# Where the late weight buffers start: 448 instead of 128 modulo 512 bytes, and steps of 64 bytes between units

## The chip, the cores and the metric

One core of a Trainium2 chip runs the whole program. The metric is the device time of one execution in microseconds, as the median of several runs.

## The reference

Attention over two sequences, then two feed-forward layers over the 1152 tokens that it gives:

```python
# attention: 2 batches, 8 heads, 576 tokens, 64 per head
scores = q @ k.T / 8, kept in a window of 32 (heads 0-3), or of 32 steps of 4 (heads 4-7)
attn = softmax(scores) @ v
x = attn as (1152, 512)
# layer 1
h = x @ w_in                       # 512 -> 2048
x = (h * tanh(softplus(h))) @ w_out   # 2048 -> 512
# layer 2: four experts, weighted by p = domain_probs / sum
for e in range(4):
    out += p[:, e] * (relu(x @ w1[e]) @ w2[e])   # 512 -> 1024 -> 512
```

## The kernel before, in words

Nearly all numbers are 32 bits wide. To keep the products exact enough at TensorE's fast 32-bit type, each operand is split in two parts, a high part (`xh`, `wxh`, `gh`, ...) and a low part (`xl`, `wxl`, `gl`, ...), and each product is three matmuls: high by high, high by low, low by high.

The order of all instructions is written out by hand (`tc.manual_schedule()`), and tiles get their places in the order in which they are declared. Pool `big` holds what lives through the whole kernel: `xh` and `xl` (18432 bytes a partition each), `wxh` and `wxl` (16384 each), `gh` and `gl` (5120 each), three buffers `raw0` to `raw2` for loads (4104 bytes, rounded up to 4128), `prob`, `psum_e`, a tile `pad` of 192 bytes that nothing reads or writes, and `scr` (18432). In the built program `xh` begins at 128 modulo 512 bytes; so do the tiles up to `raw0`, since all their sizes are multiples of 512. `raw1` begins at 160 and `raw2` at 192, and after `pad` the tile `scr` is at 128 again.

Behind `big` stands the pool `ap1` of the attention (`kk`, `qq`, `vP`, `vD`, the loaded `nat` tiles, `pr`, `pT`, `xn`). When the attention is done it is closed (`att.close()`), and the pool `wpb` takes the same bytes with the late buffers: `late0` and `late1` (1024 columns), `late2` and `late3` (11264 columns each: high and low parts) and `late4` (640). All five begin at 128 modulo 512.

There are three stages:

- **Attention**, ten units of up to 128 tokens (`Unit`, `att_step`). Beside it the weights of layer 1 are loaded and decoded (`dec_load`, `dec_dve`, `dec_act`): a DMA into one of four buffers (`raws` and a piece of `scr`), two VectorE and two ScalarE operations and a subtraction on GpSimd for each half unit.
- **Layer 1** (`Step1`). A unit is 128 of the 2048 hidden columns: 512 columns of `w_in` and 512 of `w_out`. Units 0 to 3 stand in `wxh`/`wxl`, unit 4 in `late0`/`late1`, and units 5 to 15 in `late2`/`late3`, one after the other (`unit_tiles`). The tokens go in three groups of 512, 320 and 320. `Step1.first` (line 566) multiplies by `w_in`, with the unit as the stationary operand and the tokens (`xh`, `xl`) moving; `Step1.second` (line 590) multiplies by `w_out`, with the unit stationary and the activations (`gh`, `gl`) moving. Each step runs 12 matmuls for one unit in `first` and 12 in `second`; in groups of 320 columns a step has two units.
- **Layer 2** (`Group`). Four pairs of blocks of an expert stand in `late2`/`late3`, `PW` columns apart: `prep_a` writes the first 768 columns, `prep_s` the next 1024 (sums and differences of blocks, for seven products in place of eight), `w2_hi` and `w2_lo` the last 1024 (w2). Tokens go in two sets with 256 and 320 columns a matmul. `Group.prod` (line 786) has a block of 128 columns from `late2`/`late3` as the stationary operand. `Group.second` (line 861) has 512 columns of w2 in `late2`/`late3` as the moving operand and `gh`/`gl`, `wxh`/`wxl` or `late0`/`late1` as the stationary one.

Slices of columns start at multiples of 128 columns (512 bytes), save the moving slices of the groups and sets with 320 columns, of which every second one starts 256 bytes on.

Of the kernel before, what the change touches and what calls it, by code (L numbers as in the profile page):

```python
# [8 lines left out]
F32 = mybir.dt.float32  # L9
F32R = mybir.dt.float32r  # L10
# [13 lines left out]
def kernel(  # L24
# [22 lines left out]
    NUA = 4  # L47
# [4 lines left out]

    SETS = ((0, 256), (512, 320))
    GW = 640
    PW = 2816
    EXP, MISH = "exp_and_friends", "mish"

    big = ctx.enter_context(tc.tile_pool(name="big", bufs=1))
# [23 lines left out]
    raws = [big.tile([128, 4104], U8, name=f"raw{n}") for n in range(3)]  # L82
    prob = big.tile([128, NT // 128, NE], F32, name="prob")
    psum_e = big.tile([128, NT // 128], F32, name="psum_e")
    big.tile([128, 48], F32, name="pad")

    scr = big.tile([128, NT // 128 * DM], F32, name="scr")
    hbuf = [scr[:, GW * n:GW * (n + 1)] for n in (0, 1)]
# [19 lines left out]
    late = []  # L108

    def unit_tiles(u):  # L110
        n = slice(1024 * u, 1024 * (u + 1))
        if u < NUA:
            units[u] = (wxh[:, n], wxl[:, n])
        elif u == NUA:
            units[u] = late[0:2]
        else:
            n = slice(1024 * (u - NUA - 1), 1024 * (u - NUA))
            units[u] = (late[2][:, n], late[3][:, n])

    halves = sorted(((u, p) for u in range(NF1) for p in range(2)), key=lambda h: 2 * h[0] + (2.5 if h[1] else 0))  # L120
# [42 lines left out]
    def dec_act():  # L163
        n = ndec[0]
        h = half_at(n)
        if h:

            kw = kwbuf[n % 3]
            ACT.activation(kw.bitcast(F16)[:, 1:1024:2], kw.bitcast(F32), AF.Copy)
        h = half_at(n - 1)  # L170
        if h:
            u, part = h
            if part == 0:
                unit_tiles(u)
            w, (hi, lo) = kwbuf[(n - 1) % 3].bitcast(F32), (t[:, part_cols(part)] for t in units[u])
            ACT.activation(hi, w, AF.Copy)
            POOL.tensor_tensor(out=lo, in0=w, in1=hi.bitcast(F32), op=ALU.subtract)
            dec_load()
        ndec[0] += 1
# [365 lines left out]
    class Step1:  # L545
# [27 lines left out]
        def split(self):  # L573
            ACT.activation(self.ghi, self.hc, AF.Copy)  # L574
            DVE.tensor_tensor(out=self.glo, in0=self.hc, in1=self.ghi.bitcast(F32), op=ALU.subtract)  # L575
# [29 lines left out]
    for n in (0, 1):  # L605
        o = 2 * GW * (n + 1)
# [114 lines left out]
    def prep_a(n):  # L721
        o = PW * (n % NP2)
        r = stage1.rearrange("p (c f m) -> p c f m", c=4, f=2)
        a12 = [w[:, o:o + 512].rearrange("p (c m) -> p c m", c=4) for w in late[2:4]]
        a22 = [w[:, o + 512:o + 768].rearrange("p (c m) -> p c m", c=2) for w in late[2:4]]
        split(*a12, r[:, :, 0], DVE)
        split(*a22, r[:, 2:4, 1], DVE)
        a11, a12, a21, a22 = blocks()
        POOL.tensor_tensor(out=a22, in0=a21, in1=a22, op=ALU.add)  # L729
        POOL.tensor_tensor(out=a21, in0=a11, in1=a21, op=ALU.subtract)  # L730
        POOL.tensor_tensor(out=a11, in0=a22, in1=a11, op=ALU.subtract)
        POOL.tensor_tensor(out=a12, in0=a12, in1=a11, op=ALU.subtract)

    def prep_s(n):
        o = PW * (n % NP2) + 768
        split(late[2][:, o:o + 1024], late[3][:, o:o + 1024], stage1, DVE)
        load_w1(n + 1)
        ready.add(("s", n))

    def w2_hi(n):  # L740
        o = PW * (n % NP2) + 1792
        ACT.activation(late[2][:, o:o + 1024], stage2, AF.Copy)  # L742

    def w2_lo(n):
        o = PW * (n % NP2) + 1792
        hi, lo = (t[:, o:o + 1024] for t in late[2:4])
        POOL.tensor_tensor(out=lo, in0=stage2, in1=hi.bitcast(F32), op=ALU.subtract)  # L747
        load_w2(n + 1)
        ready.add(("w2", n))
# [5 lines left out]
    def amat(name, p, k):  # L755

        o = PW * p
        o += {"A11": 128 * k, "A12": 256 + 128 * k, "A22": 512 + 128 * k, "S2": 768 + 256 * k, "S3": 896 + 256 * k,
# [3 lines left out]
    class Group:  # L762
# [90 lines left out]
        def second(self, f, which=slice(None)):  # L853
            assert ("w2", self.e * NP2 + self.p) in ready
            o = PW * self.p + 1792 + 512 * f
            wh, wl = (w[:, o:o + 512] for w in late[2:4])
# [103 lines left out]
    u1.x_lo()  # L960
    att.close()
    wpb = ctx.enter_context(tc.tile_pool(name="wpb", bufs=1))
    late += [wpb.tile([128, n], F32R, name=f"late{i}") for i, n in enumerate((1024, 1024, 11264, 11264))]
    late.append(wpb.tile([128, 640], F32, name="late4"))


# [28 lines left out]
    for e in range(1, NE):  # L995
        for p in range(NP2):
            n, g = e * NP2 + p, 2 * NP2 * (e - 1) + NP2 + p + 1
# [67 lines left out]
```

## Time and profile before

| | us |
|---|---|
| median of 3 runs | 632.76 (632.52 to 633.48) |
| the profiled execution's own time | 635.62 |
| its span, first to last instruction | 633.8 |
| TensorE busy | 625.5 (99%) |
| VectorE, ScalarE, GpSimd busy | 287.0, 261.9, 180.5 |
| mean granted TensorE clock | 0.997 of full speed |

Busy time of TensorE counts from the start of a matmul to its modelled end, and matmuls overlap. How fast a row of matmuls goes is therefore read from the chain of work that ended last: a piece with x24 is 24 matmuls that follow each other, and its length divided by 24 is the distance from start to start.

### The profile page before, as it was taken

To read this page: it belongs to the slowest core of one execution; us is meant where nothing else is said; L and a number is where in the kernel's file an instruction comes from. 1 tells how busy PE (TensorE), PEld (TensorE's weight loads), DVE (VectorE), ACT (ScalarE), POOL (GpSimd) and SP (SyncE) were. 2 spreads that over 40 slices of the span, in tenths; PEclk is the share of its full clock that TensorE was granted. 3 is DMA by queue.
4 is the path that set the end of the run, shared out by engine and by line. 5 is a ranking of instruction groups with operands and counts; after the bars stand their busy time and mean duration, and the time that the engine had idled before them with its cause. 6 is when DMAs were issued, how large, how long until landed. Compare 5 with 4: busy or idle time off the path is not lost.

```text
span 633.8 us, 10146 instructions
## 1 busy us (share of the span) xinstructions
PE 625.5 (99%) x4152; PEld 562.2 (89%) x4152; DVE 287.0 (45%) x482; ACT 261.9 (41%) x497; POOL 180.5 (28%) x201
## 2 busy tenths in 40 slices
PE   8998999999999999999999999999999999999997
PEld 5776888889999999998998899998999988989986
DVE  6887677613111333474534523444523444424223
ACT  7786777624223443452344322444322443322220
POOL 8763555512100242180243200234200335100000
PEclk9998999999999999999999999999999999999999
DMA  8865677300000122020023200123100132000102
GB/s 192 195 184 156 222 223 220 128 1 1 1 1 1 67 79 87 1 101 1 13 88 100 66 1 1 34 78 90 67 1 0 34 101 66 2 1 30 38 1 83
DMA packets 51358, 43.66 MB, mean 69 GB/s; under 512 B 26352, under 2 KB 44144, under 8 KB 51312
## 3 DMA queue, kind: packets, MB, share of 16 engines
q1 hardware_dynamic: 51312, 43.02, 22.9%
q8 instruction: 32, 0.52, 0.3%
q14 instruction: 14, 0.11, 0.1%
HBM read 40.65 MB, written 2.36 MB: 68 GB/s over the span
## 4 chain that ended last, share of the span: by engine, by line
PE 92%; DMA 3%; DVE 2%; SPq 1%; ACT 1%; POOL 0%; issue 0%; DVEq 0%; POOLq 0%
PE bank L861 31%; PE bank L786 28%; PE bank L590 16%; PE bank L566 15%; DMA raw<-in_moe_w_out_dram 1%; DMA scr<-in_moe_w_in_dram 1%; DMA vP<-in_v_dram 1%; DMA natk<-in_k_dram 1%; DVE pr L383 1%; DVE mx L382 1%; PE bank L326 0%; SPq L282 0%; PE bank L396 0%; ACT pr L384 0%; PE bank L374 0%; POOL vP L289 0%
## 5 line engine op out<-in xcount | busy, mean ns | idle before, releaser
L786 PE MATMUL bank<-xh,late 128*128 128x256 f32 (+1 forms) x512 | 120.4, 296 | 0.0
L786 PE MATMUL bank<-wxh,late 128*128 128x320 f32 (+1 forms) x384 | 94.9, 296 | 0.0
L786 PEld LDWEIGHTS bank<-xh,late 128*128 128x128 f32 x512 | 89.1, 190 | 1.8
L861 PE MATMUL bank<-late,gh 128*128 128x512 f32 x280 | 87.0, 392 | 0.0
L729 POOL TENSOR_TENSOR raw<-raw 128x256 f32<-128x256 f32 x16 | 12.2, 764 | 225.1 <-DVE late L618 225.1
L566 PE MATMUL bank<-xh,late 128*128 128x320 f32 (+1 forms) x288 | 75.9, 336 | 0.0
L786 PE MATMUL bank<-xl,late 128*128 128x256 f32 (+1 forms) x256 | 75.7, 296 | 0.0
L590 PE MATMUL bank<-gh,late 128*128 128x320 f32 (+1 forms) x288 | 72.0, 336 | 0.0
L786 PEld LDWEIGHTS bank<-wxh,late 128*128 128x128 f32 x384 | 68.5, 190 | 0.6
L575 DVE TENSOR_TENSOR gl<-scr,gh 128x512 fp32r<-128x512 f32 (+1 forms) x32 | 24.5, 767 | 80.0 <-ACT gh L574 80.0
L861 PEld LDWEIGHTS bank<-late,gh 128*128 128x128 f32 x280 | 50.9, 188 | 9.0
L571 ACT ACTIVATE scr<-bank 128x320 f32<-128x320 f32 (+1 forms) x48 | 23.5, 489 | 83.4 <-PE bank L566 83.4
L747 POOL TENSOR_TENSOR late<-raw,late 128x1024 fp32r<-128x1024 f32 x16 | 38.8, 2422 | 64.8 <-ACT late L742 64.8
L786 PE MATMUL bank<-wxl,late 128*128 128x256 f32 (+1 forms) x192 | 56.9, 296 | 0.1
L861 PE MATMUL bank<-late,gl 128*128 128x512 f32 x140 | 54.5, 389 | 0.0
L566 PEld LDWEIGHTS bank<-xh,late 128*128 128x128 f32 x288 | 50.6, 188 | 3.8
L590 PEld LDWEIGHTS bank<-gh,late 128*128 128x128 f32 x288 | 50.1, 188 | 3.7
L861 PE MATMUL bank<-late,late 128*128 128x512 f32 (+1 forms) x219 | 52.8, 388 | 0.0
L786 PEld LDWEIGHTS bank<-xl,late 128*128 128x128 f32 x256 | 48.5, 190 | 1.8
L566 PE MATMUL bank<-xl,late 128*128 128x320 f32 (+1 forms) x144 | 48.3, 336 | 0.0
L590 PE MATMUL bank<-gl,late 128*128 128x320 f32 (+1 forms) x144 | 48.3, 336 | 0.0
L861 PE MATMUL bank<-late,wxh 128*128 128x512 f32 (+1 forms) x154 | 47.4, 389 | 0.0
(153 smaller groups left out, 1137.3 us busy)
## 6 DMA issues: line engine op xcount, KB each, us to landing
raw<-in_moe_w_dram SPq DMA_DIRECT2D x32, 512.0 KB, 3.4
raw<-in_moe_w_out_dram SPq DMA_DIRECT2D x15, 512.0 KB, 3.6
raw<-in_moe_w_in_dram SPq DMA_DIRECT2D x9, 512.0 KB, 4.2
scr<-in_moe_w_in_dram SPq DMA_DIRECT2D x7, 512.0 KB, 4.9
natk<-in_k_dram SPq DMA_DIRECT2D x8, 256.0 KB, 3.5
natq<-in_q_dram SPq DMA_DIRECT2D x8, 256.0 KB, 4.0
out_dram<-scr SPq DMA_DIRECT2D x8, 256.0 KB, 2.0
vD<-in_v_dram SPq DMA_DIRECT2D x16, 64.0 KB, 4.1
```

The lines of the kernel that those rows point to most:

```text
L382: DVE.tensor_reduce(out=mx, in_=sv, axis=AX.X, op=ALU.max)
L383: DVE.tensor_tensor(out=self.pr, in0=sv, in1=mx.unsqueeze(2).to_broadcast([128, 8, 64]), op=ALU.subtract)
L566: PE.matmul(h, a[:, c, :], x[:, c, :], start=c == 0 and k == 0, stop=c == 3 and k == 2)
L571: ACT.activation(self.hc[:, self.w * i:self.w * (i + 1)], h, AF.Mish)
L575: DVE.tensor_tensor(out=self.glo, in0=self.hc, in1=self.ghi.bitcast(F32), op=ALU.subtract)
L590: PE.matmul(yacc[self.grp][d], a[:, 512 + 128 * d:640 + 128 * d], x[:, g], start=u == UORD[self.grp][0] and k == 0, stop=u == UORD[self.gr ...
L729: POOL.tensor_tensor(out=a22, in0=a21, in1=a22, op=ALU.add)
L747: POOL.tensor_tensor(out=lo, in0=stage2, in1=hi.bitcast(F32), op=ALU.subtract)
L786: PE.matmul(out, w, x(k), start=first and k == 0 and i == 0, stop=k == 1 and i == 2, skip_group_check=not first)
L861: PE.matmul(acc, x[:, s], a[:, cols], start=self.p == 0 and f == 0 and i == 0, stop=self.p == NP2 - 1 and f == 1 and i == 2, skip_group_ch ...
```

## The change

The tile `pad` goes, so that `scr`, the attention's pool and the late buffers all begin 192 bytes earlier: 448 modulo 512 in place of 128. `late2` and `late3` grow from 11264 to 11392 columns. The units in them stand 1040 columns apart (4160 bytes: 64 more than a multiple of 512) up to the ninth, and 1024 apart behind it. So the eleven units begin at 448, 0, 64, 128, 192, 256, 320, 384, 448, 448 and 448 modulo 512. An expert's pairs stand 2832 columns apart (11328 bytes, again 64 more than a multiple of 512) in place of 2816: at 448, 0, 64 and 128. The late buffers then end at 229312 bytes in place of 228480. The instructions, their order on every engine and the semaphores that each waits for stay as they were; which units' bytes a pair takes over stays the same too.

```diff
-    PW = 2816
+    PW = 2832
...
     psum_e = big.tile([128, NT // 128], F32, name="psum_e")
-    big.tile([128, 48], F32, name="pad")
...
         else:
-            n = slice(1024 * (u - NUA - 1), 1024 * (u - NUA))
+            o = 1024 * (u - NUA - 1) + 16 * min(u - NUA - 1, 8)
+            n = slice(o, o + 1024)
             units[u] = (late[2][:, n], late[3][:, n])
...
-    late += [wpb.tile([128, n], F32R, name=f"late{i}") for i, n in enumerate((1024, 1024, 11264, 11264))]
+    late += [wpb.tile([128, n], F32R, name=f"late{i}") for i, n in enumerate((1024, 1024, 11392, 11392))]
```

## Rows read from the trace of the kernel before

**Rows 1.** The page: busy tenths in 40 slices, and the granted clock.
```profile
PE   8998999999999999999999999999999999999997
PEclk9998999999999999999999999999999999999999
```

**Rows 2.** Busy time by stretch: each engine's us and instructions, clock, DMA share, GB/s.
```profile
20.00:43.00 23.00, 22.32 (x428) 18.04 (x417) 20.47 (x40) 17.39 (x33) 15.09 (x29) 1.00 0.86 213
64.00:120.00 56.00, 56.00 (x250) 46.37 (x250) 41.49 (x57) 40.20 (x67) 32.21 (x24) 1.00 0.70 222
120.00:286.00 166.00, 166.00 (x1079) 159.93 (x1078) 56.48 (x80) 64.33 (x118) 41.52 (x32) 1.00 0.10 33
286.00:293.00 7.00, 6.94 (x43) 6.20 (x42) 2.75 (x5) 2.23 (x5) 0.00 (x0) 1.00 0.00 0
293.00:480.00 187.00, 187.00 (x1098) 169.39 (x1097) 78.58 (x138) 64.34 (x127) 43.00 (x40) 1.00 0.15 46
480.00:620.00 140.00, 140.00 (x812) 127.14 (x811) 53.73 (x95) 42.38 (x87) 21.50 (x20) 1.00 0.10 31
```

**Rows 3.** The chain that ended last, in order of time: start us, us, what.
```profile
72.89 2.72 PE bank L566 x12
...
75.61 2.72 PE bank L590 x12
...
200.75 3.52 PE bank L566 x24
...
204.26 3.52 PE bank L590 x24
...
268.39 4.31 PE bank L786 x36
...
302.11 4.39 PE bank L786 x30
...
306.50 3.42 PE bank L861 x15
```

**Rows 4.** The same chain around 45 us.
```profile
37.67 7.16 DMA raw<-in_moe_w_out_dram
...
45.20 4.99 DMA scr<-in_moe_w_in_dram
...
50.29 0.43 DVE scr L152
50.72 0.60 DVE scr L159
51.31 0.61 DVE mx L382
...
51.95 0.70 DVE pr L383
...
52.67 0.64 ACT pr L384
```

**Rows 5.** TensorE in order of time around 53 us, and busy time of two stretches there.
```profile
53.36 0.66 PE L396 MATMUL bank<-ident,pr 128*128 128x128 f32 x4 [2.29 <-ACT pr L384]
...
51.00:54.00 3.00, 0.71 (x6) 0.65 (x6) 2.79 (x7) 2.11 (x4) 1.27 (x1) 1.00 0.88 248
54.00:58.00 4.00, 4.00 (x32) 2.60 (x31) 3.66 (x8) 3.83 (x6) 0.00 (x0) 0.57 0.29 93
```

**Rows 6.** Instructions that touch a late buffer, over the whole span (columns of rows 2).
```profile
0.00:634.00 634.00, 528.18 (x3078) 480.39 (x3078) 80.86 (x144) 100.62 (x184) 71.78 (x40) 1.00 0.23 69
```

**Rows 7.** Groups of weight loads by shape (names, shapes, count, busy us, mean ns).
```profile
L326 PEld LDWEIGHTS bank<-ident,natk 128*128 128x128 f32 x32 | 4.2, 159 | 1.6 <-issue 1.0 <-DMA natk<-in_k_dram 0.6
...
L429 PEld LDWEIGHTS bank<-ident,xn 128*128 128x128 f32 x36 | 3.7, 141 | 2.0 <-issue 1.9
```

**Rows 8.** Groups of matmuls by shape, line 861.
```profile
L861 PE MATMUL bank<-late,gh 128*128 128x512 f32 x280 | 87.0, 392 | 0.0
L861 PE MATMUL bank<-late,gl 128*128 128x512 f32 x140 | 54.5, 389 | 0.0
```

**Rows 9.** Groups of ScalarE and VectorE operations by shape.
```profile
L574 ACT ACTIVATE gh<-scr 128x512 fp32r<-128x512 f32 x16 | 10.1, 633 | 0.5
...
L822 ACT ACTIVATE gh<-raw 128x512 fp32r<-128x512 f32 x8 | 5.1, 632 | 7.2 <-DVE raw L806 7.2
...
L811 ACT ACTIVATE late<-bank 128x320 f32<-128x320 f32 x16 | 7.0, 437 | 6.7 <-PE bank L786 6.7
L799 ACT ACTIVATE raw<-bank 128x320 f32<-128x320 f32 x16 | 7.0, 437 | 6.8 <-PE bank L786 6.8
...
L575 DVE TENSOR_TENSOR gl<-scr,gh 128x640 fp32r<-128x640 f32 x16 | 13.2, 825 | 65.6 <-ACT gh L574 65.6
...
L823 DVE SCALAR_TENSOR_TENSOR gl<-raw,gh 128x640 fp32r<-128x640 f32 x8 | 6.6, 826 | 1.1
```

**Rows 10.** DMA issues by line: count, KB each, median us from issue to landing.
```profile
raw<-in_moe_w_in_dram SPq DMA_DIRECT2D x9, 512.0 KB, 4.2
scr<-in_moe_w_in_dram SPq DMA_DIRECT2D x7, 512.0 KB, 4.9
```

## The prediction

> **What bounds the kernel now.** I read the page first, then the busy time by stretch, then the chain of work that ended last, and only then single groups. The page says that TensorE has work nearly everywhere; no slice of it falls below eight tenths before the last [rows 1]. By stretch, TensorE is busy for all of 64 to 286 us and all of 293 to 620 us, at a granted clock of 1.00 (the level of 2.4 GHz) [rows 2]. The chain in those stretches is matmuls alone. So what counts there is the distance from one matmul to the next.
>
> That distance comes from the chain's pieces [rows 3]: 12 matmuls of 512 columns in 2.72 us are 226.7 ns each, 24 of 320 columns in 3.52 us are 146.7 ns each, 36 of 256 columns in 4.31 us are 119.7 ns each. From 256 to 512 columns it is 107 ns for 256 columns, 0.418 ns a column, which is one column per cycle of 2.4 GHz. What is left is the same at all three widths: 226.7 - 512/2.4 = 13.3 ns, 146.7 - 320/2.4 = 13.3 ns, 119.7 - 256/2.4 = 13.0 ns, about 32 cycles. Line 861 starts its pieces a little slower (3.42 us for 15 is 228.0 ns), which is 1.3 ns more.
>
> Time is lost only in the front. Of 20 to 43 us TensorE is busy 22.32 of 23 us [rows 2]. Around 51 us it idles 2.29 us for the exponential of a softmax [rows 5], and the chain shows why that was late: VectorE first had to decode a weight that landed at 50.19 us, 4.99 us after its DMA was issued, and before that a load of 7.16 us is on the chain [rows 4]. [...]
>
> **The change part by part.** No instruction is added, removed or moved, on any engine or DMA queue, and no wait. What changes is where operands begin. So each term is a count of instructions times what another start costs, and the trace has no late operand at the new starts. I bound each by the nearest rows.
>
> *Matmuls with a late operand.* There are 3078, each with one weight load [rows 6]. In 64 to 286 us and 293 to 620 us none waits for anything, so anything that a start costs here lands in the time at full size. What speaks for nothing: the moving slices of 320 columns begin in turn at 128 and 384 modulo 512, against stationary operands at 128, while those of 512 columns all begin at 128; both leave the same 13.3 ns [rows 3]. So a distance of 256 bytes between the two operands costs the same as none. For 64 bytes the nearest rows are the weight loads of the attention's transposes: `xn` begins at 448 modulo 512 and its loads take 141 ns, those of `natk` at 256 take 159 ns [rows 7], so a start at an odd multiple of 64 is not seen to be slower. I take 0. The lower end is a gain of all of the 13.3 ns, treated as a rival below. The upper end is the slowest that line 861 shows: matmuls of `late,gh` last 392 ns on average and those of `late,gl` 389 [rows 8], 3 ns more; 3 ns x 3078 = 9.2 us. I take 0, since the rows with other starts are nearer to the case than a mean over matmuls that all have one start.
>
> *ScalarE, VectorE and GpSimd on late buffers and `scr`.* 144, 184 and 40 operations touch late buffers [rows 6]. `raw2` begins at 192, so it shows a start of 64 bytes beside the rest: reading it costs ScalarE 632 ns for 512 columns, where `scr` at 128 costs 633; VectorE 826 ns against 825 for 640 columns; writing it costs ScalarE 437 ns for 320 columns, the same as `late4` at its old start [rows 9]. I take 0. Even 5% more on each (80.86 + 100.62 + 71.78 us busy, so 12.7 us in all) would be hidden: TensorE never waits for them after 293 us, and VectorE and ScalarE are busy for under half of 293 to 480 us (78.58 and 64.34 of 187) [rows 2]. Only the wait near 290 us, 0.06 us in the busy column, is open to them.
>
> *The attention's tiles and their loads.* They begin 192 bytes earlier, at multiples of 64 bytes off the old starts. Their matmuls and copies are covered by the same rows. For their loads the trace has one pair: the same 512 KB of `w_in` land in 4.2 us in `raw` and in 4.9 us in `scr` [rows 10]. That is a difference of place in the queue as much as of address. I take 0, with 0.7 us a load as the bound either way for the loads on the chain.
>
> *Columns added to `late2` and `late3`.* Nothing reads or writes them; the pairs take over the same units as before. 0.
>
> The sum is 0. The profiled execution took 635.62 us, 2.86 above the median of the three runs, so I put the sum on the median: 632.76 + 0, **632.8 us**. Three runs span 0.96 us, so I count 0.2% (1.27 us) either way as what a measurement can tell from no change.
>
> **The rivals.**
>
> *Late starts cost TensorE a little (slower).* The place is lines 566, 590, 786 and 861, where the moving stream and the next weight load read at the same time. With starts that step by 64 bytes the two meet at distances that the trace doesn't have. The price is that of the 3078 matmuls. It decides from 0.41 ns each (1.27 us / 3078), which is one column of 2.4 GHz: 634.0 us. At 3 ns it would be 642 us. I think the low end likelier, one to two columns: 634.0 to 635.3. For it: no row has these distances, and TensorE has no slack to hide them. Against it: a distance of 256 bytes and other starts cost nothing.
>
> *The 13.3 ns are a clash that the new starts end (faster).* If operands that begin alike hold each other up for 32 cycles, seven of eight starts would be free of it: 3078 x 13.3 ns x 7/8 = 35.8 us, so 597 us. Against it: the 13.3 ns are alike for moving starts of 128 and of 384, and for 256, 320 and 512 columns, which a clash of two streams would hardly be [rows 3]; they look like a fixed price of each weight load. [...]
>
> *The front shifts (either way).* The stall near 51 us hangs on two DMAs. If the load into `scr` lands in 4.2 us as those into `raw` do, the stall shrinks by 0.8 us, and if the clock then holds, 54 to 58 us need 4 x 0.57 = 2.3 us in place of 4: 2.5 us in all, 630.3. If it takes another 0.7 to 2.2 us (up to the 7.16 us that the load before took), 633.5 to 635.0.
>
> *The change doesn't do what it says.* The sizes give the starts directly (192 bytes less; 4160 and 11328 are 64 above multiples of 512), so I leave this no chance of its own; it would give 632.8 too.
>
> **How the numbers follow.** No change: 0.68. Late starts cost: 0.14. The front slower: 0.06, faster: 0.08. The clash ends: 0.04. So slower by over 0.2%: 0.20; faster: 0.12; within: 0.68. The range reaches at the bottom over most of the front's gain (631.0, where all of it would be 630.3), and at the top over its loss (635.0) and over two columns a matmul (635.3): 631.0 to 635.4. Left out are the clash, the best case of the front and the dear end of late starts, about 0.13 in all.
>
> **What would show it.** Right: in the changed kernel's chain a piece of 24 at 3.52 us, 36 at 4.31, 12 at 2.72, 15 at 3.42, and operations on late buffers at the old mean times. The step on matmuls is wrong if any of those pieces is longer or shorter by over 0.01 us; then its price is that difference over the count. The step on the front is wrong if the first piece of 12 of line 566 behind the attention starts earlier or later than at 72.89 us by over 1 us while the pieces stay. If pieces and front both stay and the time moves, something that I have not named is at work.

## The result, and the profile after

The changed kernel takes 636.66 us (636.44 to 637.01, 4 runs) against 633.12 us before (632.52 to 633.98, 4 runs): a ratio of 1.0055, with an interval of 1.0038 to 1.0073. It is 3.5 us slower. 632.8 us was forecast, with a range up to 635.4.

| | before | after |
|---|---|---|
| the profiled execution's own time, us | 635.62 | 637.01 |
| its span, us | 633.8 | 635.2 |
| TensorE busy, us | 625.5 | 627.9 |
| mean granted clock | 0.997 | 0.999 |

The two profiles differ by only 1.4 us, because the profiled execution of before was a dear one: it stood 2.5 us above its median and has the stall of 2.29 us and the granted clock of 0.57 near 54 us [rows 4, 5]; the one of after has TensorE busy for 3.00 of 3.00 us from 51 to 54 us and a clock of 1.00 from 54 to 58 us. So the front of the two can't be compared piece by piece from these two profiles alone. The rest can, and there the loss shows. The chain of the changed kernel in layer 1, in the first group of tokens (start us, us, what):

```profile
71.63 2.80 PE bank L566 x12
74.43 2.75 PE bank L590 x12
...
82.78 2.80 PE bank L566 x12
...
88.37 2.75 PE bank L566 x12
...
93.90 2.72 PE bank L566 x12
...
99.37 2.80 PE bank L566 x12
...
110.52 2.79 PE bank L566 x12
...
116.10 2.74 PE bank L566 x12
...
135.53 2.80 PE bank L590 x12
138.33 3.52 PE bank L566 x24
```

And of the kernel before, where its pieces of 320 columns begin, where layer 2 begins, and the last piece:

```profile
138.17 3.52 PE bank L566 x24
...
250.03 3.60 PE bank L786 x30
...
619.92 10.31 PE bank L861 x51
```

Before, all of these pieces of 12 were 2.72 us [rows 3]. Now most are 2.74 to 2.80. The pieces of 320 columns are still 3.52. From 71.63 us to 138.33, where the first piece of 320 columns begins, there are 66.70 us; before, from 72.89 to 138.17, 65.28 us for the same 24 pieces. That is 1.42 us more.

The same chain in layer 2:

```profile
250.18 3.54 PE bank L786 x30
...
530.26 3.42 PE bank L786 x30
...
537.81 3.49 PE bank L861 x15
541.30 4.24 PE bank L786 x36
...
562.34 4.28 PE bank L786 x36
...
598.39 4.39 PE bank L786 x30
602.78 3.48 PE bank L861 x15
...
621.12 10.49 PE bank L861 x51
```

Here it goes both ways. Line 861 (512 columns) takes 3.42 to 3.50 us for 15 where it took 3.42 [rows 3], line 786 with 256 columns takes 4.24 to 4.28 for 36 where it took 4.31, and line 786 with 320 columns (30 in 4.39) is the same. From 250.18 to the last piece's start at 621.12 it is 370.94 us, before 369.89 (from 250.03 to 619.92), and the last piece is 10.49 against 10.31: 1.23 us more in all. Layer 1 and layer 2 together: 2.65 us of the 3.5. Such a stretch repeats closely: in the kernels below whose late buffers keep the distances of before, the one of layer 2 is 369.89 to 369.91 us.

ScalarE, VectorE and GpSimd take nearly what they took on late buffers. Groups by shape of the changed kernel (mean ns after the busy us):

```profile
L811 ACT ACTIVATE late<-bank 128x320 f32<-128x320 f32 x16 | 7.0, 439 | 6.6 <-PE bank L786 6.6
...
L822 ACT ACTIVATE gh<-raw 128x512 fp32r<-128x512 f32 x8 | 5.1, 634 | 7.0 <-DVE raw L806 7.0
```

437 and 632 ns before [rows 9]: 2 ns more. VectorE takes 492 ns for 320 columns at line 813, as before, and GpSimd 2428 ns at line 747, before 2422. The one wait of TensorE for them, near 290 us, is as long as before: from 286 to 293 us TensorE is busy for 6.95 us, before for 6.94 [rows 2].

### The profile page after: what moved, and what is told of

Read it like the earlier page. It is cut to its first block, busy times and chain, and to the rows that moved or that the text cites. A ratio compares the mean times of both kernels' runs of the same rounds, so it can differ in the third digit from the quotient of the medians.

```text
span 635.2 us, 10146 instructions
## 1 busy us (share of the span) xinstructions
PE 627.9 (99%) x4152; PEld 560.5 (88%) x4152; DVE 288.8 (45%) x482; ACT 263.0 (41%) x497; POOL 181.1 (29%) x201
## 2 busy tenths in 40 slices
DMA packets 51358, 43.66 MB, mean 69 GB/s; under 512 B 26352, under 2 KB 44144, under 8 KB 51312
## 4 chain that ended last, share of the span: by engine, by line
PE 95%; DVE 2%; ACT 1%; DMA 1%; issue 0%; SPq 0%; DVEq 0%; ACTq 0%
PE bank L861 32%; PE bank L786 28%; PE bank L590 16%; PE bank L566 16%; PE bank L326 1%; DMA natk<-in_k_dram 1%; PE bank L396 1%; PE bank L366 1%; PE bank L374 1%; PE bank L429 1%; DVE pr L383 1%; DVE mx L382 1%; ACT pr L384 0%; PE bank L412 0%; PE bank L408 0%
## 5 line engine op out<-in xcount | busy, mean ns | idle before, releaser
L786 PEld LDWEIGHTS bank<-xh,late 128*128 128x128 f32 x512 | 88.5, 188 | 2.0
L747 POOL TENSOR_TENSOR late<-raw,late 128x1024 fp32r<-128x1024 f32 x16 | 38.8, 2428 | 65.3 <-ACT late L742 65.3
```

The source lines that it names most:

```text
L786: PE.matmul(out, w, x(k), start=first and k == 0 and i == 0, stop=k == 1 and i == 2, skip_group_check=not first)
```

## Experiments

The theories. **A**: what TensorE takes from one matmul to the next hangs on the distance d between the start of the next stationary operand and the start of the moving one, modulo 512 bytes. **B**: the attention's loads land later, because their places are 64 bytes off multiples of 128. **C**: neither, only spread. An edit that adds or takes out lines shifts the line numbers behind it.

What suggests A is the row of layer 1 above. Line 566 takes the units in order, with `xh` and `xl` at 128: unit 4 (d=320) 2.80 us, unit 6 (d=384) 2.80, unit 7 (d=448) 2.75, unit 8 (d=0) 2.72, unit 9 (d=64) 2.80, unit 11 (d=192) 2.79, unit 12 (d=256) 2.74.

### The start alone

```diff
-    big.tile([128, 48], F32, name="pad")
```

> The tile pad goes and nothing else: everything behind it begins at 448 modulo 512, units and pairs stay whole multiples of 512 bytes apart. Theory A (distance): what TensorE takes from one matmul to the next hangs on d, the start of the next stationary operand minus the start of the moving one, modulo 512. In the changed kernel 512-column matmuls cost 0 more at d=0 and 256 and about 6.5 ns more at 64, 192 and 320; 256-column ones cost 5 to 7 ns less at 320; 320-column ones nothing. Here: in layer 1 all late 512-column steps are at d=320, 12 matmuls in 2.80 us (before 2.72); 36 of 256 columns at d=320 in about 4.1 us (before 4.31); 15 of 512 in layer 2 at d=192 in about 3.50 us (before 3.42). Sum +1.9 - 4.0 + 2.9 = +0.8 us. Theory B (front): the loss is in the attention, whose tiles and loads stand 64 bytes off multiples of 128; pieces stay at 2.72, 4.31, 3.42, the front comes 1 to 2 us later. If both hold: 634 to 635.5 us against 633.1. Theory C (the chip's spread): same as before, 632.5 to 634, with no piece changed.

Measured: 635.67 us against 633.24 in the runs beside it, ratio 1.0034 (1.0021 to 1.0046). Its chain:

```profile
75.92 2.80 PE bank L565 x12
...
257.17 4.09 PE bank L785 x36
...
277.76 4.24 PE bank L785 x36
...
305.32 3.45 PE bank L860 x15
...
493.06 3.43 PE bank L860 x15
```

and of the changed kernel, whose first pair has d=192 too:

```profile
306.69 3.44 PE bank L861 x15
```

The pieces move as A said, in both directions: 2.80 in layer 1, 4.09 to 4.24 for 256 columns. Here all late units begin alike, so it isn't the step from one unit to the next that costs. Line 860 (861 of before) stayed nearer to before (3.43 to 3.45) than the 3.50 expected; that expectation had the price too high, for the changed kernel's own piece at d=192 takes 3.44. And 256 columns at one distance show two levels: 4.09 and 4.11 in the first two pieces, 4.24 in those behind. With line 590 at 74.43 us above, 2.75 us at d=0 between two pieces of late units (2.72 before [rows 3]), this shows that d alone doesn't settle the time of a piece; that its neighbours matter too is the author's reading.

### The step of the pairs alone

```diff
-    PW = 2816
+    PW = 2832
...
-    late += [... (1024, 1024, 11264, 11264) ...]
+    late += [... (1024, 1024, 11328, 11328) ...]
```

> The tile pad stays, all starts at 128; only the pairs of layer 2 stand 2832 columns apart, so pairs 0 to 3 begin at 128, 192, 256, 320. Theory A: layer 1 as before; 512-column matmuls of pairs 0 to 3 at d=0, 448, 384, 320: +0, +2 to 3, +2 to 5, +6.5 ns; 256-column ones at d=0, 64, 128, 192: 0 and, for the three that no run has shown yet, somewhere between 0 and -7 ns. With half of that, 504 x -3 = -1.5 us and 640 x 4 = +2.5 us less what the starts of pieces cost before: 633 to 635 us. Theory B: the front is untouched, so 633.1, the same as before. The front's first piece of line 566 should not come later in either.

Measured: 634.56 us against 633.24, ratio 1.0020 (1.0009 to 1.0032). One thing differs from the text above: 11328 columns are 88.5 times 512 bytes, so `late3`, the low halves, began at 384 and not at 128. In layer 1 the low halves of the units were thus at d=256. Their pieces:

```profile
71.68 2.72 PE bank L566 x12
...
305.34 3.44 PE bank L861 x15
...
318.37 3.45 PE bank L861 x15
...
331.43 3.48 PE bank L861 x15
...
343.75 3.50 PE bank L861 x15
...
540.45 4.24 PE bank L786 x36
544.69 2.75 PE bank L861 x12
...
550.88 4.27 PE bank L786 x36
555.15 2.80 PE bank L861 x12
```

So d=256 costs 512 columns nothing here, where a third of the matmuls of a late unit have it; where all have it, in unit 12 of the changed kernel, the piece takes 2.74 us. Pair 0, with d=0 and 256, keeps 2.75 us for 12 at line 861; the next has 2.80. In the sets of 320 columns line 861 gives 3.44, 3.45, 3.48 and 3.50 us for the pairs 0 to 3, whose high halves have d=0, 448, 384 and 320: the order that A expected.

### The front alone

```diff
-    big.tile([128, 48], F32, name="pad")
...
+    wpb.tile([128, 48], F32, name="pad")
     late += [wpb.tile([128, n], F32R, name=f"late{i}") ...]
```

> The tile pad moves from the end of pool big to the head of the late pool: the attention's tiles and scr begin at 448 as in the change, all late buffers at 128 as before. Theory A alone: nothing late moves, so the time of before, 633.1 us, and all pieces as before. Theory B: the attention's loads land later (medians of 4.0, 4.3 and 4.2 us for natk, natq and vP, as in the change, against 3.5, 4.0 and 3.6) and the whole kernel is 1 to 2 us slower: 634.1 to 635.1 us. If A and B share the loss of 3.5 us, about 634.3.

Measured: 634.33 us against 633.24, ratio 1.0015 (1.0002 to 1.0028). All pieces in the late part are those of before (2.72 for 12, 4.31 for 36). So some 1.0 us belongs to the front, apart from any late buffer; the interval reaches from 0.1 to 1.8 us. Busy time from 20 to 43 us, of this kernel (the last two numbers are the busy share of the DMA engines and GB/s):

```profile
20.00:43.00 23.00, 22.30 (x404) 18.07 (x402) 19.59 (x41) 18.03 (x36) 14.85 (x29) 1.00 0.95 213
```

and of the changed kernel:

```profile
20.00:43.00 23.00, 22.46 (x425) 18.18 (x427) 20.03 (x39) 17.51 (x35) 14.91 (x30) 1.00 0.94 214
```

Before it was 0.86 at the same 213 GB/s [rows 2]: the engines are busy for a tenth longer to move the same bytes.

### The blocks of line 786 alone

In this layout w2 of the four pairs stands first in `late2` and `late3`, and the blocks of line 786 stand behind it, 80 columns further on.

```diff
-        o = PW * (n % NP2)
+        o = at_a(n % NP2)          # 4176 + 1792 * pair
...
-        o = PW * (n % NP2) + 1792
+        o = 1024 * (n % NP2)
...
-            n = slice(1024 * (u - NUA - 1), 1024 * (u - NUA))
+            k = SLOT[u - NUA - 1]  # (4, 5, 0, 1, 6, 7, 2, 3, 8, 9, 10)
+            n = slice(1024 * k, 1024 * k + 1024)
```

> Before, with only the blocks of line 786 moved: w2 of the four pairs stands first in late2 and late3 (at 128 modulo 512), the blocks of all pairs behind them 80 columns further on, at 448. Units stay at 128, in another order of places so that pairs come free at the same steps. Theory A: 512-column matmuls keep d=0; 256-column ones go to d=320 and take 5 to 6.7 ns less each: 672 x 5 to 6.7 = 3.4 to 4.5 us faster, 628.6 to 629.8 us, 36 of them in about 4.08 us in place of 4.31. Theory B or C: 633.1, no piece changed.

Measured: 637.43 us against 633.24, ratio 1.0054 (1.0037 to 1.0071), the opposite of what was expected. The layout was not what the text says: 11344 columns for `late2` put `late3` at 448, and with it the low halves of units and w2. Where only the blocks were meant to move, a third of the matmuls of layer 1 and of line 861 moved as well, and the pieces of 12 in layer 1 became 2.76 to 2.79:

```profile
95.76 2.76 PE bank L591 x12
98.52 2.79 PE bank L567 x12
```

The low halves of the blocks went to d=128 and not to 320. The run decides nothing about the blocks; it shows that one of three operands off the free distances is enough to slow a piece. With `late2` at 11392 columns, so that `late3` begins at 128:

> The layout of e4_blocks_448, with late2 widened to 11392 columns so that late3 begins at 128 too (in e4 it began at 448, so the low halves of units and w2 had moved as well, which was not meant). Units and w2 at 128, blocks of line 786 at 448 in both. Theory A (distance): 512-column pieces as before (12 in 2.72 us, layer 1 costs nothing more), 256-column ones at d=320: 36 in 4.23 us at the 2.3 ns less that e1 showed (4.08 at 6.7 less), 672 x 2.3 = 1.5 us faster at the least, 4.5 at the most: 628.7 to 631.7 against 633.2. Theory D, a rival after e4: leaving 128 anywhere in the late buffers costs, whatever the distance: then 633.2 or slower, with 512-column pieces at 2.75 us or more.

Measured: **632.01 us** against 633.53, ratio 0.9972 (0.9961 to 0.9982), faster than the kernel before. Its chain:

```profile
133.18 2.72 PE bank L591 x12
...
255.38 4.09 PE bank L790 x36
...
536.84 4.24 PE bank L790 x36
541.08 2.75 PE bank L865 x12
```

Line 591 and line 865 (lines 590 and 861 of before) have the pieces of before, and 36 of 256 columns take 4.24 us in place of 4.31 (4.09 in the first such piece), as at d=320 in the first experiment. That is the low end of what was expected. D falls: the blocks of line 786, which only matmuls of 256 and 320 columns use, may leave 128.

### Distances between multiples of 64 bytes

The same layout with the blocks of the pairs at 4104 + 1808 columns a pair.

> As e5_both_448, but the blocks of pairs 0 to 3 begin 32, 96, 160 and 224 bytes past 128 modulo 512: d = 32, 96, 160, 224 for 256 columns, none of which a run has shown. Theory A: units and w2 as before. If only 64-byte lines count, 32 behaves as 0 or 64 and so on: 0 to 2.3 ns less each; if finer places count, the four pairs differ in another way. 631 to 633.2 us.

Measured: 633.33 us, one run. Pieces of 36 with 256 columns, of pairs 0 and 1, 1 and 2, 2 and 3:

```profile
537.92 4.27 PE bank L790 x36
...
548.41 4.29 PE bank L790 x36
...
558.93 4.21 PE bank L790 x36
```

All are under the 4.31 of d=0 and none is under 4.20. A piece holds 6 matmuls of the one pair and 30 of the other; the fastest is the one with 30 at d=224. Whether the place within 64 bytes counts isn't shown. The same distance (224) for all pairs:

> As e5_both_448, with the blocks of line 786 224 bytes past 128 modulo 512 (at 352) for all four pairs, the distance at which 256 columns went fastest in e6 (3.0 ns less on average, 2.3 less at d=320). Theory A: 36 of 256 columns in 4.20 us (4.23 in e5, 4.31 before), 672 x 0.7 = 0.5 us less than e5: 631.4 against 632.0 there, and some 2 us under the kernel before. If the rest of e6's gain belonged to the way in which its pairs followed each other: the time of e5.

Measured: 631.74 us against 633.41, ratio 0.9975 (0.9965 to 0.9985), with 36 in 4.20 us:

```profile
536.02 4.20 PE bank L790 x36
```

From the version at d=320 it can't be told apart by time; they beat the kernel before by 1.7 and 1.5 us.

### Everything shifted together

```diff
+    big.tile([128, 16], F32, name="pad0")
     xh = big.tile([128, 4 * NT], F32R, name="xh")
```

> Before, with 64 bytes ahead of xh: every tile of the kernel, the late ones too, begins 64 bytes later, at 192 modulo 512 where it was at 128. All distances between moving and stationary operands stay. Theory A (distance counts, not the start): every piece on TensorE as before (2.72, 3.52, 4.31, 3.42 us). Rival A2 (a start off multiples of 128 bytes costs in itself): pieces of 512 columns at 2.75 to 2.80 us. Theory B: nat at 320, again 64 off a multiple of 128, so the front costs 1.1 us as in e3_front_only. A with B: 634.3 us; A2 with B: 637 us or more.

Measured: 634.39 us against 633.53, ratio 1.0009 (0.9998 to 1.0021), so by time alone not clear of no change. Its chain and its front:

```profile
73.72 2.72 PE bank L591 x12
...
244.61 3.52 PE bank L591 x24
...
535.12 3.43 PE bank L862 x15
538.54 4.31 PE bank L787 x36
542.86 2.75 PE bank L862 x12
```

```profile
20.00:43.00 23.00, 22.53 (x446) 18.36 (x434) 19.90 (x39) 17.30 (x33) 15.62 (x30) 1.00 0.94 217
```

Every piece is that of before although every start is 64 bytes off. A2 falls: in these runs the pieces on TensorE go with the distance (2.72 us here, 2.80 where one of the two operands moved), not with the start. The DMA share, however, is 0.94 again, against 0.86 before [rows 2]: for the loads it goes with the start.

### The front's loads, taken apart

Three kernels move only tiles of the attention. All have 128 modulo 512 for `scr` and the late buffers.

```diff
+    ap1.tile([128, 32], F32, name="pad1")
     kk = ap1.tile([128, 4, 2, 128 * (NCH + 1)], F32, name="kk")
...
+    ap1.tile([128, 32], F32, name="pad2")
     sel = {n: ap1.tile([64, 128], BF16, name=f"sel{n}") for n in "nsf"}
```

> Before, with 128 bytes more ahead of the attention's tiles and 128 more ahead of its loaded tiles: nat at 0 and vP and vD at 256 modulo 512, in place of 256 and 128; late buffers and scr where they were. Theory B (loads into places 64 bytes off a multiple of 128 land later): these are multiples of 128 before and now, so no change, 633.2 us and the same landing times. If 256 bytes are what counts, vP lands in under 2.9 to 3.6 us and the front comes up to 0.5 us earlier: 632.7.

Measured: 633.26 us against 633.53, ratio 0.9996 (0.9984 to 1.0007): no change, as B said for places that are multiples of 128. Next, 64 bytes ahead of the loaded tiles:

```diff
     warm = ap1.tile([128, 128], BF16, name="warm")
+    ap1.tile([128, 16], F32, name="pad1")
```

> Before, with 64 bytes ahead of the attention's loaded tiles alone: nat begins at 320 modulo 512 (64 off a multiple of 128) in place of 256, while kk, qq, vP, vD, scr and all late buffers stay at 128. Theory B, told by loads: q and k take longer to land (natk and natq medians near 4.0 and 4.3 us in place of 3.4 to 3.5 and 4.0), the first matmul of line 566 comes about 0.5 to 1 us later and the whole is 0.5 to 1.1 us slower: 633.9 to 634.6 against 633.4. Rival B2 (what costs in the front is the start of matmul operands, not of loads): no change.

Measured: 634.56 us against 633.41, ratio 1.0016 (1.0007 to 1.0025). And 64 bytes ahead of `kk`, `qq`, `vP` and `vD`, with 64 more ahead of `nat`:

> The counterpart: 64 bytes ahead of kk, qq, vP and vD (192 modulo 512 in place of 128) and 64 more ahead of nat, which stays on a multiple of 128 (384). Loads of q and k are as before, loads of v go 64 off. Theory B: only v's loads land later (vP near 4.2 us in place of 2.9 to 3.6), which the front mostly hides: 633.4 to 634.0 against 633.4. Rival B2 (operands cost): 634.5, as in e3_front_only, with q's and k's landing times as before.

Measured: 634.43 us, ratio 1.0016 (1.0006 to 1.0026), more than B was expected to give. Busy time from 20 to 43 us, of the three in this order:

```profile
20.00:43.00 23.00, 22.32 (x426) 17.82 (x414) 19.72 (x39) 16.97 (x31) 15.35 (x29) 1.00 0.88 221
```

```profile
20.00:43.00 23.00, 22.47 (x446) 18.38 (x434) 20.03 (x39) 17.45 (x33) 15.67 (x30) 1.00 0.93 215
```

```profile
20.00:43.00 23.00, 22.32 (x418) 17.99 (x420) 20.13 (x40) 17.52 (x36) 15.89 (x30) 1.00 0.93 216
```

In the third kernel only v's loads are off, and yet the loads of k and q land a little late too (median 3.9 and 4.3 us). One set of loads that holds up the rest would explain this and why the two prices don't add: each kernel costs what the front alone did, about 1.0 us. That is argued and not shown. B2 isn't excluded by these times: in the second kernel `nat` itself and `pr`, `pT` and `xn` behind it are operands of TensorE and moved too, and no run moves operands of the attention without loads. What speaks for the loads is that B2 would have left their share and landing times alone. In all 13 profiles, the seven with these loads on multiples of 128 have a share of 0.83 to 0.88 here, and the six with some of them 64 bytes off have 0.93 to 1.00, all at 212 to 221 GB/s. The medians from issue to landing, in five of the seven and in all six, are 3.3 to 3.8 against 3.8 to 4.5 us for k's loads of 256 KB, and 4.0 to 4.2 against 4.2 to 5.1 for q's. The 1.0 us itself stands only in the medians of many executions: the profiled execution of the second kernel, with its 0.93, took 632.93 us, less than the median of before. Where in the front the time goes, no run shows.

## Why the prediction was wrong

The step that failed first is the one on matmuls with a late operand: "I take 0", since "a distance of 256 bytes between the two operands costs the same as none". The row that it rested on was one of 320 columns, the only ones before with a distance of 256 [rows 3], and 320 columns turned out to take 3.52 us for 24 at every distance tried. So it could say nothing of 512 columns. For these, 0 costs nothing [rows 3] and 256 little or nothing (2.72 to 2.74 us for 12); the change made six other distances, and these cost up to 80 ns for 12 matmuls (2.72 to 2.80 us), 6.7 ns each. The same step took all matmuls alike. In fact 512 columns lose, 320 columns neither lose nor gain, and 256 columns gain (4.31 to 4.24 us is 2 ns each). The rival "late starts cost TensorE a little" had the distances, the place and, at 2.65 us / 3078 = 0.9 ns on average, nearly the price (one to two columns of 0.42 ns), but only 0.14 of the chance. That the mean came out so near is luck in part: it is left over from up to 7 ns more on 512 columns, nothing on 320 and some 2 ns less on 256. The 2.4 in the prediction's sums is the rate of columns that the pieces give, 107 ns for 256 columns [rows 3]; that a column is one cycle is the author's estimate. The weight loads of `xn` and `natk` [rows 7], taken as the nearest rows for 64 bytes, say how long one load takes; the distance to the stream beside it isn't in them. Of late rows at new distances there was none, and "no row has these distances, and TensorE has no slack to hide them" should have weighed more than a pair that happened to be alike.

The second step that failed is the one on the attention's loads, also taken as 0. Its bound was drawn from one pair of landing times, 4.2 and 4.9 us [rows 10]; four other profiles with `scr` and the loads at multiples of 128 have `scr` anywhere from 0.7 us ahead of `raw` (3.9 and 4.6 us, the step of the pairs alone) to 0.3 us behind it (4.5 and 4.2, the first run with the blocks moved), so the pair said little of the address. The new places in the front, 64 bytes off multiples of 128, cost about 1.0 us. With 2.65 us on TensorE this makes 3.65 us, where 3.5 was measured; the intervals are wider than so close a fit.

The step on ScalarE, VectorE and GpSimd held where TensorE could have felt it. The columns added cost nothing that shows: with `late2` at 11392 columns and all but the blocks at 128, line 591 has its 2.72 us for 12. The front's stall near 51 us, which carried the rival of either sign, was a trait of that one execution as far as the clock tells: its mean granted clock is 0.997, that of the six other profiles with these loads on multiples of 128 is 0.999 to 1.000; from 43 to 74 us it is 0.94, and 1.00 in the versions at d=320 and 224. That the profiled execution stood 2.86 us above the median was said, but the front's rows were then used as if they were usual.

The rival "the 13.3 ns are a clash that the new starts end" was wrong by size, and for 512 columns by sign, but 256 columns did gain: 30 matmuls at 530.26 us take 3.42 us, 114 ns each, 6 ns less than before. So the rest beside the columns is no fixed price of a weight load. And where the two operands start counts: 12 matmuls of 512 columns take 2.72 or 2.80 us by it. Whether the moving stream and the weight load meet, and where, no run shows.

What stays open is how d makes its price. The distance is shown to count (everything shifted: 2.72 us for 12 as before; one operand moved: 2.80), but one distance can have two levels, as 4.09 and 4.24 us at d=320. That it also depends on what ran before is the author's estimate from these two; no run looked inside that. Nor is it shown that the next stationary operand counts and not the current one, which in most of these rows begin alike.

## What to carry to other kernels

When a kernel's bound is a dense row of matmuls, the starts of its moving and stationary operands relative to each other are a parameter like any other: in this kernel 0 modulo 512 bytes was best for 512 columns (2.72 us for 12; 2.72 to 2.74 at 256) and 224 or 320 for 256 columns (4.20 and 4.24 us for 36, 4.31 at 0); check such distances by the chain, and look after every change of a tile's size where the tiles behind it have gone to. Look at the places that many small DMAs write to as well: here those 64 bytes off multiples of 128 cost about 1.0 us, with a DMA share of 0.93 to 1.00 in place of 0.83 to 0.88. And a profile that stands well above the median, as this one by 2.5 us, tells little about the stretch in which it lost the time.

## What the runs showed of the hardware that was not expected

- The time from one matmul of 512 columns to the next is 226.7 ns at d=0, some 229 ns at 256 and 448, and up to 233 ns at the other multiples of 64 (2.72, 2.75 and 2.80 us for 12); at 192 it was anything from 229 to 233 (3.44 us for 15, 2.79 for 12).
- With 256 columns it is the other way round: 119.7 ns at d=0 (4.31 us for 36), 117.8 at d=320 (4.24), and 114 in some pieces (3.42 us for 30).
- With 320 columns, whose moving slices begin 256 bytes apart in turn, no distance changed more than some 0.02 us a piece (3.51 to 3.52 us for 24 in all kernels).
- Loads, most of them of 256-byte rows (26352 of the program's 51358 packets are under 512 bytes), into places 64 bytes off multiples of 128 keep the DMA engines busy for 0.93 to 1.00 of a stretch in which they are busy for 0.83 to 0.88 otherwise, at the same GB/s.
